# Gated linear attention in front of a mixture of experts: the attention stage rewritten around an order computed by a list scheduler

## The chip, the cores and the metric

The kernel runs on one core of one Trainium2 chip. The core has five engines with a queue each: PE (matrix products), DVE (vector), ACT (scalar and activation), POOL (GpSimd) and SP, which here only issues transfers. They work at once and wait for one another by semaphores. The metric is device microseconds of one execution: the median of several runs. The profile is one separate execution.

## The reference

The attention is a recurrence over 768 tokens, for 4 sequences and 8 heads of 48 channels. The experts take its output; every token goes to one of 8 experts, with 384 tokens for each, assigned greedily by logit.

```python
for t in range(S):                                   # S = 768, D = 48
    state = alpha[:, :, t, :, None] * state + einsum('bhd,bhe->bhde', k[:, :, t], v[:, :, t])
    y[:, :, t] = einsum('bhd,bhde->bhe', q[:, :, t], state)

x = y.transpose(0, 2, 1, 3).reshape(B * S, H * D)    # 3072 x 384
logits = x @ w_gate                                  # 8 experts
order = argsort(-logits.flatten())                   # token, expert; full experts and assigned tokens skipped
for e in range(E):
    h = maximum(x[mask_e] @ w1[e], 0)                # 384 -> 1024
    out[mask_e] = h @ w2[e]                          # 1024 -> 384
```

## The kernel before

**Steps.** The attention works in chunks of 128 tokens. A step `s` takes two heads (one above the other in 64-partition halves) and four chunks; `g, p = divmod(s, 4)` names the group of four chunks and the pair of heads. There are 24 steps, and every sixth chunk ends a sequence. One step loads four arrays of 256 KB (`load`, `load_v`, on SP's queue, three steps ahead, four buffers each) and does:

- `decay` (L221 to L224): a backward scan of `alpha` on DVE gives `sc`, a reciprocal of each chunk's first value goes into `d1f`, and a forward scan gives `ga`. The scans are 517 wide, each chunk padded to 129, so that a zero stops the running product at its end. Both of a scan's operands lie in SBUF.
- `scale_k` on DVE (L229) and `scale_q` on POOL (L235): `kh = k * sc`, `qh = q * ga`.
- `keys` (L241, L243): four transposes of `kh` on PE, copied out by ACT as `kn`.
- `scores` (L250): eight products of 64 rows on PE; `causal` (L258, L259): per head a copy by ACT and a triangular mask in place on POOL.
- `states` (L269): the products of keys and values of each chunk; `carry` (L282, L287, L289): DVE adds them to the decayed state of the pair, and ACT writes the decayed state into a block-diagonal tile `sb`, one instruction for each chunk and head, 160 in all.
- `outputs` (L296, L302): the carried state by `qh`, then the scores by the values, into one PSUM bank `y`; `emit` (L310) copies it out as `yt`.
- `logits` (L315 to L320): four products with the gate's weights into PSUM, added by DVE into `lt`. After each group `choose` transposes `lt` (L329), and `first_choice` (L351 to L364) finds each token's best expert and the first digit of its key; `first_counts` (L376) counts.
- `y_trans` (L339, L342): the rows of x are transposed back, copied by ACT into `xg`, and stored to DRAM on ACT's queue. These are put off: `fill` places them behind the last steps, and the search of the first expert waits for some of them in each level (`Y_IN_SEARCH`).

PSUM has eight banks: two for transposes (`psx`), four for the scores (two heads, two buffers), one for `y`, and one shared by states, logits and counts.

**Order.** The loop over `s` is written by hand, with steps two and one behind interleaved, and the framework orders each engine's queue by it. The first two steps run in halves on DVE (`first`, L407 to L414). `init_route` builds the tables of the routing between the steps.

**After the attention.** For each expert a search finds the threshold digit by digit in five levels: a compare (L503), 24 counting products (L551), a threshold (L552). `extract` makes the token list, rows are gathered by indirect DMA (L699), and `ffn1` and `ffn2` (L768, L788) run with weights split in two parts. The first threshold of the first expert (L379) needs the last logits.

Of the kernel before, what the change touches and what calls it, by code (L numbers as in the profile page):

```python
# [12 lines left out]
ROUTE_AHEAD = 3  # L13
LAST_BLOCKS = 2
WARM_UP = 10
Y_IN_SEARCH = (3, 4, 4, 3)
WARM_IN_ROUTE = (6, 4, 2, 2)
Y_BEFORE_CHOICE = 1
Y_BEFORE_LOGITS = 2
Y_BEFORE_COUNTS = 5  # L20
I32 = mybir.dt.int32
AF = mybir.ActivationFunctionType
OP = mybir.AluOpType


@with_exitstack
def gla_moe_kernel(ctx, tc, q, k, v, alpha, w_gate, w1, w2, out):
# [70 lines left out]
    def init_route():  # L98
        ib = dict(allow_small_or_imprecise_dtypes=True)
        nc.gpsimd.iota(ramp, pattern=[[-1, E]], base=E, channel_multiplier=0, **ib)  # L100
        nc.gpsimd.iota(pcol, pattern=[[0, 1]], base=0, channel_multiplier=1, **ib)
        tc.keep_in_program_order(
            nc.gpsimd.iota(iota, pattern=[[1, T], [0, U]], base=1, channel_multiplier=0, **ib))
        sh = 32
        for t, bits in enumerate(BITS):
            sh -= bits
            nc.any.memset(shifts[:, t], sh)
            nc.any.memset(masks[:, t], 2 ** bits - 1)
            nc.any.memset(scale[:, t], SC8[t])
        yield  # L110
        nc.vector.tensor_copy(ramp_b, ramp[:, None, :].to_broadcast([128, NU, E]))
        nc.any.memset(ones_c, 1.0)
        nc.any.memset(rem, float(CAP))
        nc.any.memset(pen, 0.0)
        nc.any.memset(asg, 0.0)
        yield
        nc.gpsimd.iota(cst, pattern=[[128, NU], [0, NB]], base=-N // 2, channel_multiplier=1, **ib)
        nc.gpsimd.iota(bsel, pattern=[[0, NU], [1, NB]], base=0, channel_multiplier=0, **ib)
        for t in range(nb):
            nc.gpsimd.memset(onet[t], SC8[t])  # L120
        nc.vector.tensor_scalar(pcs, pcol, SC8[nb - 1], None, op0=OP.mult)
        yield
        nc.gpsimd.affine_select(tri, ones, pattern=[[1, 128]], compare_op=OP.is_gt, fill=0.0, base=0,
                                channel_multiplier=-1)
        for c in cbuf:
            for w in range(0, NW, 2):
                tc.keep_in_program_order(nc.gpsimd.memset(c[:, w:w + 2], 0.0))
            yield
        for t in range(1, nb):
            n = iotas[t].shape[1]  # L130
            tc.keep_in_program_order(
                nc.vector.tensor_scalar(iotas[t], iota[:, :n], SC8[t], None, op0=OP.mult))
            yield
# [737 lines left out]
```

## Time and profile before

| | us |
|---|---|
| median of 3 runs (lowest, highest) | 475.99 (474.95, 479.57) |
| the profiled execution, its own time | 481.46 |
| its span, first to last instruction | 479.8 |
| last copy of `y` out of PSUM begins (L310) | 164.54 |
| first threshold of the first expert (L379) | 169.60 |
| first gather of rows (L699) | 190.45 |
| PE busy (3982 instructions) | 420.2 |
| DVE busy (868) | 291.4 |
| ACT busy (524) | 265.4 |
| POOL busy (181) | 183.2 |

How to read it: the profiled execution is one run, longer than its span by 1.7 us at the ends. Busy time of an engine is the sum of its instructions' records; on PE these overlap, since products are pipelined. A group's row gives its line and engine, output and inputs, the count, then the busy time and the mean in ns, then the engine's idle time in front of the group and what ended it. A timeline row gives start, length, engine, line, and the idle time before it in brackets. A row of waits gives who waited for what, the sum, the count and the longest.

### The profile page before, as it was taken

The numbers are of one execution on the slowest core, as the hardware profiler recorded it, in microseconds if no ns is written. First come the engines' busy times: TensorE is split into PE (matmuls) and PEld (weight loads), VectorE is DVE, ScalarE is ACT, GpSimd is POOL, SyncE is SP. The second block draws the span as 40 slices with busy tenths as digits, with TensorE's granted clock in tenths as the row PEclk, the third lists the DMA queues.
The fourth block names the chain that finished last, engine by engine and source line by source line (L and its number), as shares of the span: only waits on it lengthen the run. The fifth ranks groups of instructions, "written<-read, shape, count | busy, mean of one in ns | idle before, by whom it ended". The sixth has DMA issues, their size and how long they took to land.

```text
span 479.8 us, 10370 instructions
## 1 busy us (share of the span) xinstructions
PE 420.2 (88%) x3982; PEld 368.3 (77%) x3982; DVE 291.4 (61%) x868; ACT 265.4 (55%) x524; POOL 183.2 (38%) x181
## 2 busy tenths in 40 slices
PE   5987877888778885699899999988998999999993
PEld 3765756676657674489889998978986999999993
DVE  7998887788884257438768585774774851212210
ACT  2576677677587652562845637463444467674311
POOL 2765754567453100310542547045043135251202
PEclk8599789888998997669999999997997999999998
DMA  7566555545570067888999999998696599997201
GB/s 256 163 181 196 153 177 176 154 151 170 149 194 2 12 253 259 176 197 231 242 211 301 198 242 309 196 305 179 166 269 173 124 313 309 260 235 133 67 0 49
DMA packets 53296, 90.33 MB, mean 188 GB/s; under 512 B 3840, under 2 KB 27392, under 8 KB 53248
## 3 DMA queue, kind: packets, MB, share of 16 engines
q0 software_dynamic: 11776, 34.61, 34.0%
q1 hardware_dynamic: 38304, 50.35, 33.1%
q10 hardware_dynamic: 3168, 4.72, 2.7%
q8 instruction: 31, 0.51, 0.4%
q14 instruction: 17, 0.14, 0.1%
HBM read 55.06 MB, written 9.44 MB: 134 GB/s over the span
## 4 chain that ended last, share of the span: by engine, by line
PE 56%; DVE 14%; DMA 12%; issue 9%; ACT 4%; POOL 2%; another core or an unknown queue 1%; SPq 0%; POOLq 0%; ACTq 0%; DVEq 0%
PE h L768 19%; PE y L788 17%; PE rt L551 5%; DMA al<-in_alpha_dram 5%; DVE sc L221 4%; PE y L302 3%; PE y L296 3%; DVE ga L224 2%; DMA raw_k<-in_k_dram 2%; DMA w1lo<-w1r 2%; PE xt L339 1%; PE xt L752 1%; DMA w1r<-in_moe_w_dram 1%; PE s L250 1%; DVE st L289 1%
## 5 line engine op out<-in xcount | busy, mean ns | idle before, releaser
L772 ACT ACTIVATE hh<-h 128x384 fp32r<-128x384 f32 x64 | 31.0, 487 | 85.4 <-PE h L768 72.5
L773 DVE SCALAR_TENSOR_TENSOR hl<-h,hh 128x384 fp32r<-128x384 f32 x64 | 35.4, 554 | 62.7 <-ACT hh L772 58.6
L282 ACT ACTIVATE sb<-st,sc 64x48 f32<-64x48 f32 x160 | 53.1, 332 | 30.1 <-DVE st L289 12.1
L259 POOL TENSOR_SCALAR_AFFINE_SELECT sm<-sm 128x512 f32<-128x512 f32 x48 | 43.4, 924 | 67.7 <-ACT sm L258 67.7
L788 PE MATMUL y<-w2hi,hh 128*128 128x384 f32 x192 | 67.3, 350 | 1.5 <-ACT hh L772 1.5
L788 PE MATMUL y<-w2hi,hl 128*128 128x384 f32 x192 | 66.7, 348 | 0.0
L788 PE MATMUL y<-w2lo,hh 128*128 128x384 f32 x192 | 66.4, 346 | 0.0
L768 PE MATMUL h<-xh,w1lo 128*128 128x384 f32 x192 | 49.9, 361 | 1.6 <-DMA w1lo<-w1r 1.6
L699 POOL DMA_INDIRECT xr<-x_dram,idx x24 | 31.3, 1306 | 52.3 <-DVE val L630 31.2
L799 POOL DMA_INDIRECT out_dram<-yt,idx x24 | 28.2, 1174 | 60.4 <-ACT yt L792 55.5
L768 PE MATMUL h<-xl,w1hi 128*128 128x384 f32 x192 | 49.0, 357 | 0.0
L768 PE MATMUL h<-xh,w1hi 128*128 128x384 f32 x192 | 48.2, 355 | 0.2 <-ACT w2lo L728 0.2
L727 ACT ACTIVATE w1hi<-w1r 128x768 fp32r<-128x768 f32 x32 | 26.8, 839 | 35.8 <-DMA w1r<-in_moe_w_dram 14.2
L732 POOL DMA_DIRECT2D w1lo<-w1r x16 | 22.1, 1379 | 56.0 <-ACT w1lo L728 44.3
L768 PEld LDWEIGHTS h<-xh,w1lo 128*128 128x128 f32 x192 | 36.4, 201 | 5.8 <-issue 3.7
L788 PEld LDWEIGHTS y<-w2hi,hh 128*128 128x128 f32 x192 | 36.8, 192 | 2.6 <-ACT hh L772 1.8
L768 PEld LDWEIGHTS h<-xl,w1hi 128*128 128x128 f32 x192 | 35.9, 199 | 2.8 <-issue 2.6
L788 PEld LDWEIGHTS y<-w2lo,hh 128*128 128x128 f32 x192 | 37.0, 193 | 0.0
L788 PEld LDWEIGHTS y<-w2hi,hl 128*128 128x128 f32 x192 | 36.9, 192 | 0.1
L221 DVE TENSOR_TENSOR_SCAN sc<-al,d1r 128x517 f32<-128x517 f32 x22 | 32.7, 1486 | 6.0 <-DMA al<-in_alpha_dram 3.2
L302 PE MATMUL y<-sm,vt 128*48 128x128 f32 (+1 forms) x384 | 36.2, 312 | 0.0
L768 PEld LDWEIGHTS h<-xh,w1hi 128*128 128x128 f32 x192 | 35.4, 197 | 1.0 <-ACT w2lo L728 0.6
(171 smaller groups left out, 874.7 us busy)
## 6 DMA issues: line engine op xcount, KB each, us to landing
w1r<-in_moe_w_dram SPq DMA_DIRECT2D x16, 768.0 KB, 8.1
w2r<-in_moe_w_dram SPq DMA_DIRECT2D x16, 768.0 KB, 7.2
w1lo<-w1r POOLq DMA_DIRECT2D x16, 768.0 KB
w2lo<-w2r POOLq DMA_DIRECT2D x16, 768.0 KB
al<-in_alpha_dram SPq DMA_DIRECT2D x24, 256.0 KB, 3.3
raw_k<-in_k_dram SPq DMA_DIRECT2D x24, 256.0 KB, 5.3
raw_q<-in_q_dram SPq DMA_DIRECT2D x24, 256.0 KB, 4.0
vt<-in_v_dram SPq DMA_DIRECT2D x24, 256.0 KB, 2.6
```

Of the source, the lines that this page charges most:

```text
L221: nc.vector.tensor_tensor_scan(sc[:, ::-1], a[:, ::-1], d1r[:, ::-1], 1.0, op0=OP.mult, op1=OP.add)
L259: nc.gpsimd.affine_select(SM[s][:, h], SM[s][:, h], pattern=[[0, 4], [1, C]], compare_op=OP.is_ge, fill=0.0, base=0, channel_multiplier=-1)
L282: nc.scalar.activation(SB[s, u][hs, h, :D], St[p][hs], AF.Copy, scale=ac[hs])
L302: yield lambda u=u, h=h, n=n: nc.tensor.matmul(o[64 * h:64 * h + n, u], VT[s][:, u, h, :n], SM[s][:, h, u], start=False, stop=(u == 3), sk ...
L551: nc.tensor.matmul(cnt, cmp[:, j // U, :, j % U], o[:, j], start=(j == 0), stop=(j == NU - 1))
L699: last_gather[0] = nc.gpsimd.indirect_dma_start(out=XR[i][:, b], out_offset=None, in_=x_dram, in_offset=bass.IndirectOffsetOnAxis(ap=IDX[i ...
L727: nc.scalar.activation(hi[ix_], raw_[ix_], AF.Copy)
L768: nc.tensor.matmul(o, a[:, d], x[:, d], start=(n == 0), stop=(n == 3 * DB - 1))
L772: nc.scalar.activation(hh, o, AF.Relu)
L773: nc.vector.scalar_tensor_tensor(hl, o, 0.0, hh, op0=OP.max, op1=OP.subtract)
L788: F2[i, q] = nc.tensor.matmul(Y[b], a[:, bs], w, start=(q == 0 and n == 0), stop=(q == FB - 1 and n == 2))
L799: st_ = nc.gpsimd.indirect_dma_start(out=out, out_offset=bass.IndirectOffsetOnAxis(ap=IDX[i][:, b:b + 1], axis=0), in_=yt, in_offset=None)
```

## The change

The attention stage is written again, as a list of operations with an engine, an assumed cost, and the data each reads and writes. The list is ordered by a scheduler that runs while the program is built, and the order is kept as it is on all five queues (`manual_schedule` with PE, DVE, ACT, POOL and SP). The experts' stage is unchanged but for the search of the first expert, which no longer waits for row transposes.

The scheduler gives every operation a rank (the longest path behind it, plus `pl.base`, 4.4 us for each step still to come) and, going forward in time with the assumed costs, starts on each engine the operation of highest rank among those that can start within 0.1 us of the first. Buffers are rings that are handed out in the same pass.

```diff
+class Plan:
+    def add(self, eng, cost, fn, r=(), w=(), lat=None, port=False):
...
+    def order(self):
...
+            rank[i] = cost + max([rank[j] + (lat if ops[j][0] != eng else 0.0) for j in after[i]], default=0.0)
+        rank = [x + op[7] for x, op in zip(rank, ops)]
...
+            eng, t0 = min(((e, min(x)[0]) for e, x in first.items()), key=lambda x: x[1])
+            t, i = min(((t, i) for t, i in first[eng] if t <= t0 + SLACK), key=lambda x: (-rank[x[1]], x[0]))
...
+HOP = {"PE": 0.3, "DVE": 0.15, "ACT": 0.2, "POOL": 0.2, "SP": 2.2}
+SLACK = 0.1
```

Buffers and banks. PSUM now holds one bank for all transposes (`xt`: keys, rows, logits and counts), one for small products `m` (`dvb`), two for the scores of both heads, one each for `y`, states and logits, and one for the scan's second operand `zb`.

```diff
+    RA, RK, RQ = (ring(6, [128, w], n) for n, w in (("al", AW), ("rk", 4 * C), ("rq", 4 * C)))
+    RV = ring(6, [128, 4, 2, D], "rv")
+    TE, TP = ring(3, [128, 4 * C], "te"), ring(2, [128, 4 * C], "tp")
+    KH, QH = ring(3, [128, 4, C], "kh"), ring(4, [128, 4, C], "qh")
+    KN, SM = ring(2, [128, 4, C], "kn"), ring(2, [128, 2, 4, C], "sm")
+    SB = ring(2, [128, 4, 2, 64], "sb")
+    YT, XG = ring(4, [128, 4, C], "yt"), ring(2, [128, 4, Dm], "xg")
...
+    XT = Kind([bank("xt", [128, 4, C], psx)], ordered=False)
+    dvb = bank("xt", [128, 4, C], psx).rearrange("p a b -> p (a b)")
+    SC, YB, ST, LG = (Kind([bank(n, [128, x, 4, C] if x > 1 else [128, 4, C])])
+                      for n, x in (("s", 2), ("y", 1), ("st", 1), ("lg", 1)))
+    zb = bank("z", [128, 4 * C])
+    MR = Kind([dvb[:, 12 * i:12 * i + 12].rearrange("p (u c) -> p u c", c=3) for i in range(6)])
```

Scans and scaling. The host sets the first `alpha` of each chunk to zero, so the scans are 512 wide without padding, and hands the true first values over in 12 more columns of the same array. The first two steps run in halves; `kh` and `qh` are made on DVE for step 0 and on POOL after it.

```diff
+            def scan_e(lo=lo, top=top):
+                nc.vector.tensor_tensor_scan(te.t[:, lo:top][:, ::-1], al.t[:, lo + 1:top + 1][:, ::-1],
+                                             zb[:, lo + 1:top + 1][:, ::-1], 1.0, op0=OP.mult, op1=OP.add)
+            def scan_p(lo=lo, hi=hi):
+                nc.vector.tensor_tensor_scan(tp.t[:, lo:hi], al.t[:, lo:hi], zb[:, lo:hi], 1.0,
+                                             op0=OP.mult, op1=OP.add)
+            def ends(us=us, lo=lo, hi=hi, n=n):
+                a0 = al.t[:, 4 * C + 1:4 * C + 13].rearrange("p (u c) -> p u c", c=3)
+                nc.vector.tensor_tensor(m.t[:, us], a0[:, us], te.t[:, lo:hi:C][:, :, None].to_broadcast([128, n, 3]),
+                                        op=OP.mult)
...
+            ek, ck, en = (V, 0.08 + 0.15 * n, nc.vector) if s == 0 else (G_, 0.06 + 0.28 * n, nc.gpsimd)
+            add(ek, ck, lambda f=mul: f(en, kh, rk, te), r=each_u(te) + [rk], w=each_u(kh), port=True)
...
+            add(ek, ck, lambda f=mul: f(en, qh, rq, tp), r=each_u(tp) + [rq], w=each_u(qh), port=True)
...
+                add(V, 0.08, lambda: nc.vector.memset(zb[:, 0:4 * C:C], 1.0), w=["Z"])
```

Scores, states, outputs. One ACT copy and one POOL mask cover both heads. The states of a pair stay in five slots of one tile, and one DVE product of the slots by `m` (whose columns hold the decay for the upper head, the lower head and both) writes all eight blocks of `sb`.

```diff
+        add(P_, 0.45, turn(xt, kh), r=[(kh, u) for u in every], w=[xt])
+        add(A_, 0.6, lambda: nc.scalar.activation(kn.t, xt.t, AF.Copy), r=[xt], w=[kn])
...
+            add(P_, 0.45, score, r=[(kh, u) for u in us2] + [(qh, u) for u in us2], w=[(sc, a)])
+        add(A_, 1.05, lambda: nc.scalar.activation(sm.t, sc.t, AF.Copy), r=[(sc, 0), (sc, 1)], w=[sm])
+        add(G_, 1.15, lambda: nc.gpsimd.affine_select(
+            sm.t, sm.t, pattern=[[0, 8], [1, C]], compare_op=OP.is_ge, fill=0.0, base=0, channel_multiplier=-1),
+            w=[sm])
...
+                    slot(u + 1), slot(u), m.t[:, u, 2:3], st.t[:, u, :D], op0=OP.mult, op1=OP.add),
+                    r=[st, m], w=[("T", p)])
+        def carried():
+            t = ts[:, 4:0:-1] if g % 2 else ts[:, 0:4]
+            nc.vector.tensor_tensor(sb.t[:, :, :, :D], t[:, :, None, :].to_broadcast([128, 4, 2, D]),
+                                    m.t[:, :, :2, None].to_broadcast([128, 4, 2, D]), op=OP.mult)
...
+        add(A_, 0.6, lambda: nc.scalar.activation(yt.t, yb.t, AF.Copy), r=[yb], w=[yt])
```

Logits, rows, choice. The logits of the four pairs accumulate in PSUM and are copied once by ACT. The rows of x are transposed in each step and stored on SP's queue after each group. The choice runs in three batches (`BATCHES = ((0, 3), (3, 5), (5, 6))`, in groups) in place of six, with the compare written into the search's own buffer.

```diff
+                nc.tensor.matmul(lg.t[32 * u:32 * u + 32, 0], wg[:, p], yt.t[:, u], start=(p == 0),
+                                 stop=(p == HP - 1), skip_group_check=True)
...
+            add(P_, 0.45, turn(x3, yt), r=[yt], w=[x3])
...
+                add("SP", 3.0, lambda: nc.sync.dma_start(
+                    x_dram[4 * g * C:4 * (g + 1) * C].rearrange("(u p) d -> p u d", p=C), xg.t),
...
-                    head[0] += Y_IN_SEARCH[t - 1]
-                    order = [last_k[0], YM[head[0] - 1]]
+                    order = [last_k[0]] if last_k[0] else []
```

On the host, `v` is no longer padded (48 columns a head in place of 64), and `alpha` has 528 columns in place of 512.

More of the change, by code (lines that the diff above doesn't have):

```diff
@@ L118, in init_route @@
[L118 to L128, printed above, removed]
+            a("POOL", 0.1, lambda t=t, sh=sh: gp.memset(shifts[:, t], sh))
@@ L461, in gla_moe_kernel @@
+    ordered = dict(engines={mybir.EngineType.PE, mybir.EngineType.DVE, mybir.EngineType.Activation,
+                            mybir.EngineType.Pool, mybir.EngineType.SP})
+    with tc.manual_schedule(**ordered):
+        pl.issue()
+    if DEBUG:
+        DEBUG(pl)
     att.close()
```

624 lines of the change are left out of this document (318 added, 306 removed).

## The prediction

> **What bounds the kernel now.** I read first the page's heading and slices, then the table of stretches, then the groups of instructions of the steady part, the waits of SP's queue, and last the timeline of single blocks. The table of stretches cuts the span where the work changes: start, steady attention, attention's tail, first search, experts. Columns: the stretch, its length, busy time of each engine (instructions), granted clock, DMA share, GB/s.
>
> ```profile
> span 479.8 us, 10370 instructions
> 10.00:20.00 10.00, 9.60 (x66) 7.15 (x66) 9.90 (x22) 5.85 (x13) 8.41 (x18) 0.50 0.83 266
> 20.00:140.00 120.00, 98.68 (x1250) 79.09 (x1249) 100.08 (x220) 83.15 (x202) 69.56 (x62) 0.89 0.57 165
> 140.00:166.00 26.00, 21.57 (x267) 17.34 (x262) 11.07 (x36) 18.14 (x45) 6.92 (x8) 0.93 0.09 26
> 190.50:479.80 289.30, 267.82 (x2180) 248.29 (x2178) 147.50 (x486) 146.85 (x240) 95.88 (x80) 0.94 0.81 204
> ```
>
> The change touches only what lies before 190.5 us. From 20 to 140 us no engine is full: PE's records cover 82%, DVE 83%, and PE's records overlap one another. What sets the pace shows in the groups of 20 to 140 us, the waits of SP's queue, and the first chain row:
>
> ```profile
> L282 ACT ACTIVATE sb<-st,sc 64x48 f32<-64x48 f32 x126 | 41.9, 332 | 23.6 <-DVE st L289 10.6 <-DVE d1f L222 4.8 <-DVE val L353 2.7
> L259 POOL TENSOR_SCALAR_AFFINE_SELECT sm<-sm 128x512 f32<-128x512 f32 x38 | 36.8, 987 | 47.0 <-ACT sm L258 47.0
> L235 POOL TENSOR_TENSOR qh<-raw_q,ga 128x512 f32<-128x512 f32 x20 | 32.4, 1618 | 3.5 <-issue 2.6 <-PE y L296 0.7
> L221 DVE TENSOR_TENSOR_SCAN sc<-al,d1r 128x517 f32<-128x517 f32 x21 | 31.5, 1499 | 6.0 <-DMA al<-in_alpha_dram 3.2 <-ACT sm L258 1.5 <-ACT sb L282 1.2
> L224 DVE TENSOR_TENSOR_SCAN ga<-al,d1f 128x517 f32<-128x517 f32 x20 | 30.3, 1516 | 0.0
> L258 ACT ACTIVATE sm<-s 128x512 f32<-128x512 f32 x38 | 20.8, 600 | 0.9 <-PE s L250 0.7
> L229 DVE TENSOR_TENSOR kh<-raw_k,sc 128x512 f32<-128x512 f32 x20 | 17.9, 896 | 1.7 <-DMA raw_k<-in_k_dram 1.7
> L289 DVE SCALAR_TENSOR_TENSOR st<-st,sc,st 128x48 f32<-128x48 f32 x49 | 12.2, 249 | 2.0 <-PE st L269 1.8
> L320 DVE TENSOR_TENSOR lt<-lt,st 128x128 f32<-128x128 f32 x14 | 3.9, 278 | 5.7 <-PE st L315 5.7
> L222 DVE RECIPROCAL d1f<-sc 128x4 f32<-128x4 f32 x20 | 3.5, 173 | 0.1
> SPq L182 <- PE y L302: 77.4, 18, 8.7
> by line: DMA al<-in_alpha_dram 16.5%; DVE sc L221 11.9%; PE y L302 10.4%; PE y L296 9.2%; DVE ga L224 8.0%; DMA raw_k<-in_k_dram 7.2%; issue 5.4%; DVE st L289 3.9%; PE st L269 3.8%; ACT sb L282 3.7%; PE st L315 3.7%; DVE kh L229 2.7%; PE s
> ```
>
> Some 20 steps (20 of the 24 `ga` scans) in 120 us make 6.0 us a step. It is a loop over four engines: SP's load of `vt` waits for `outputs` of an older step on PE (77.4 us in 18 waits), the `al` load is queued behind it, the next scan waits for that, and PE, ACT and DVE hand one step on to the next. DVE's own work is about 5.0 us a step (100.08 / 20), and half a microsecond of that is contention, as the timeline shows:
>
> ```profile
> 142.69 1.22 DVE L224 TENSOR_TENSOR_SCAN ga<-al,d1f 128x517 f32<-128x517 f32 x1
> 147.04 1.21 POOL L235 TENSOR_TENSOR qh<-raw_q,ga 128x512 f32<-128x512 f32 x1 [0.30 <-PE y L296]
> 147.12 1.15 DVE L355 TENSOR_SCALAR sg<-m 128x4 int32<-128x4 int32 x1
> ```
>
> A scan alone takes 1.22 us against 1.50 on average; a four-element instruction took 1.15 us because POOL's product began just before it.
>
> **The change part by part.** *PE.* It keeps every attention product, and the 24 row transposes (`y_trans`), most of which ran between 160 and 183 us, move into the steps. The price of a block is the start of the next minus its own start, where they follow without a wait, at full clock (timeline of PE, 154 to 161 us):
>
> ```profile
> 154.63 0.66 PE L241 MATMUL xt<-ident,kh 128*128 128x128 f32 x4
> 155.22 1.16 PE L250 MATMUL s<-qh,kh 64*128 64x128 f32 x16
> 157.08 0.42 PE L315 MATMUL st<-yt,wg 128*32 128x128 f32 x8 [0.70 <-ACT yt L310]
> 157.44 0.94 PE L296 MATMUL y<-qh,sb 128*128 128x128 f32 x6
> 158.30 0.47 PE L269 MATMUL st<-vt,kn 128*48 128x48 f32 x12
> 158.71 0.49 PE L296 MATMUL y<-qh,sb 128*128 128x128 f32 x2
> 159.12 1.08 PE L302 MATMUL y<-sm,vt 128*48 128x128 f32 x16
> 160.13 1.09 PE L339 MATMUL xt<-ident,yt 128*128 128x128 f32 x8
> ```
>
> Over 24 steps: key transposes 0.59 x 24 = 14.2; scores 1.16 x 24 = 27.8; logits 0.36 x 24 = 8.6; carried products 0.86/6 x 160 records (80 chunks carry a state, two records a product) = 22.9; states 0.41/12 x 320 = 10.9; scores by values 1.01 x 24 = 24.2; row transposes 1.09/8 x 96 = 13.1. Sum 122 us, 5.07 a step. The lower bound is the weight loads' own time, 79.09/20 = 4.0 a step, plus 0.55 for the row transposes: 4.5, or 109 us. I take 122: the gaps between blocks of unlike shape recur in the rows wherever the shape changes, and the change keeps the shapes.
>
> *DVE.* Removed: `kh` (0.90; now on POOL from the second step), `lt` (0.28; logits accumulate in PSUM), contention on two scans. Added: the product that makes `m` (`ends`), a memset, `carried`. A step: scans 2 x 1.22, reciprocal 0.17, `ends` 0.17 (the row nearest in size is the reciprocal), memset 0.1 (under the reciprocal), states 3.33 x 0.25 = 0.83, `carried` with 384 elements between `lt`'s 0.28 (128) and `kh`'s 0.90 (512, contended), taken 0.5. That is 4.2, or 100 us; the s=0 products 1.8, three batches of choice (about 33 small instructions at 0.17 and the wide compare) 8, six table instructions at 0.5 or less, 2.5: 112. That a scan reads its second operand from PSUM at the old price no row shows; the bounds are 1.22 (alone) and 1.50 (as now), so 0 to +13 us; I take 0, since `lt` at 128 elements with a PSUM operand costs 0.28, of one kind with SBUF rows.
>
> `ends` still takes two SBUF operands. Bounds from the rows above: 0, or a wait for a whole POOL product, 24 x 1.2 = 29 us. I take a third, 10. DVE 122 us.
>
> *POOL.* `kh`, `qh`, one wide mask: 2 x 1.21 plus twice the mask's shortest, 0.63:
>
> ```profile
> L259 POOL TENSOR_SCALAR_AFFINE_SELECT sm<-sm x48: 632/692/1568, 11.6 to 158.7; 128x512 f32<-128x512 f32 x48
> L235 POOL TENSOR_TENSOR qh<-raw_q,ga x21: 1177/1609/2228, 23.1 to 147.0; 128x512 f32<-128x512 f32 x21
> ```
>
> 3.7 a step, 89 us; at today's contended means (1.62, 1.62, 2 x 0.99) 5.2, 125 us. Off the path at the first. *ACT* loses 160 `sb` instructions (160 x 0.332 = 53 us) and keeps two mask halves, `kn` and `yt` at 0.6 and the rows' copy at 0.5: 2.9 a step, covered.
>
> ```profile
> L243 ACT ACTIVATE kn<-xt 128x512 f32<-128x512 f32 x19 | 11.3, 595 | 0.3
> 165.12 0.49 ACT L342 ACTIVATE xg<-xt 128x384 f32<-128x384 f32 x1
> ```
>
>
> *DMA.* Loads are now 128 x (528+512+512+384) x 4 B = 0.99 MB a step, 23.8 MB, and x's six stores (4.7 MB) move from ACT's queue and the search into the steps, on SP's queue. The queue's row (packets, MB, share of 16 engines) gives the rate:
>
> ```profile
> q1 hardware_dynamic: 38304, 50.35, 33.1%
> ```
>
> 50.35 MB in 33.1% of 479.8 us is 317 GB/s, so 28.5 MB take 90 us, hidden under 122. Six buffers in place of four let loads run five steps ahead, which covers a store of x that waits for its rows at the head of SP's queue; the 77 us of `vt` waits lose their effect.
>
> *Start and tail.* The last rows needed, from the timeline: the first score, `yt` of the last step, the first threshold, the second search level and the first gather.
>
> ```profile
> 7.47 0.88 PE L250 MATMUL s<-qh,kh 64*128 64x128 f32 x8 [2.24 <-DVE qh L414]
> 164.54 0.60 ACT L310 ACTIVATE yt<-y 128x512 f32<-128x512 f32 x1 [1.86 <-PE y L302]
> 169.60 0.17 DVE L379 TENSOR_TENSOR g<-st,need 128x8 bf16<-128x8 f32 x1 [1.11 <-PE st L376]
> 173.96 1.03 DVE L503 TENSOR_TENSOR cmp<-nd,iota 128x768 bf16<-128x768 bf16 x2
> 175.50 0.94 PE L551 MATMUL rt<-o,cmp 128*128 128x8 bf16 x24
> 190.45 1.17 POOL L699 DMA_INDIRECT xr<-x_dram,idx  x1 [31.15 <-DVE val L630]
> ```
>
> The first step is still halved on DVE, so PE starts near 7.5. It starts cold: the row of 10 to 20 us has clock 0.50. The bounds of that cost are 0 and half of 7.5 to 20 us, 6; I take 6, since PE has steps waiting from the second on. PE's waits for others I put at 5 us (4% of 122); the bounds are 0 and the third rival below. The last `yt` then ends at 7.5 + 122 + 6 + 5 + 0.6 = 141.1, less logits and row transposes behind it (0.36 + 0.55): 140.2, against 165.1 now. Gain 24.9. DVE stands just under: 4.4 + 122 + one step's chain of some 7 = 133. From `yt` to the threshold (169.60) lie the same steps as now, 4.5 us.
>
> In the search the compare ends at 174.99 and the counts start at 175.50, behind row transposes; without them three levels save 0.5 each, 1.5. Their cover for the clock goes too: 24 counts take 0.94, twice that at half clock, in four levels 0 to 3.8 us more. I take 0, since the search's own products and the spins before the experts remain. The gather at 190.45 keeps 20 us from the last store of x, so the store moves nothing.
>
> *The sum.* 24.9 + 1.5 = 26.4 less than the profiled execution's 481.5 (span 479.8 and 1.7 around it): 455. That execution lies 5.5 above the median of the runs shown, 475.99, so the median should be 476 - 26 = **450 us**.
>
> *Two rules weighed.* DVE's contention: the rows are the scan at 1.22 or 1.50 and the 1.15 us behind POOL. The Trainium skill, "SBUF — State Buffer", section "Who interferes with whom", says that a VectorE instruction with at most one SBUF input stays clear of GpSimd, while one with two SBUF inputs waits for the whole GpSimd instruction. By it the scans go at 1.22, as in my sum, but it speaks against `ends`, where it gives the second rival. The clock: the row is 9.60 us of PE work in 10 at clock 0.50. The skill's "TensorE: Matmul & The Clock Gate", Part 1, has the clock full after one busy window of about 3.4 us; by that the 6 us fall away and the time would be 444. This case's row disagrees, so I keep the 6.
>
> **The rivals.** *First: PE packs tighter, 435 us.* If the gaps between unlike blocks close when nothing waits, PE needs 4.5 a step, 109 us, and DVE without stalls on `ends` 112. The change ranks its work by 4.4 us a step. The last `yt` comes at 4.4 + 112 + 7, plus waits of 2: 125, 40 less; with the search 41. For it: no engine's hard work is over 4.7. Against: the gaps stand in every row above.
>
> *Second: DVE becomes the bound, 463 us.* If `ends` waits for POOL's product each time, DVE needs 112 + 29 = 141, and `yt` ends at 4.4 + 141 + 7 = 152: 13 less. For it: the 1.15 us row; POOL is busy 3.7 of each 5 us, and `qh` becomes ready just as `ends` does. Against: whoever is first goes first, and `ends` needs only DVE's own work.
>
> *Third: slower, 490 us.* PSUM becomes single: scores of both heads had two buffers and get one, the transposes' two banks become one, and both transposes of a step share it. PE then stops for ACT's evictions unless another block is ready in its fixed order. The price: 1.1 (mask copy), 0.6 (`kn`), 0.5 (rows), 0.6 (`yt`), 2.8 us a step if none is covered. It decides at 6.1 a step, where PE works 5.07 of it: with 1.0 uncovered the gain is gone; with 1.6 uncovered the step is 6.7, 24 x 0.6 = 14 us over now. For it: PE works only 4.5 of 6.0 today, with more PSUM. Against: today's waits are the load loop's, and ACT sheds 2.2 us a step.
>
> **How the numbers follow.** Chances: forecast (441 to 460) 0.50; first rival 0.20; second 0.12; no gain, 471 to 481, the third rival at its turning point, 0.10; third rival above 481, 0.08. A measurement of this kernel tells about 1% from no change: faster by over 1% is 0.82, within 1% 0.10, slower 0.08. The range leaves out the no-gain and slower cases: 428 to 468, which takes in the first two rivals.
>
> **What would show it.** Right: PE records over 90% in 30 to 130 us at clock 1.0, steps of 5.0 to 5.3 us, scans at 1.2, no wait of SP for PE products in front of loads, the last `yt` near 140 and the first gather near 164. First rival: steps of 4.5. Second: `ends` with a mean near 1 us. Third: PE's idle time put down to ACT `sm`, `kn` or `yt`. The prediction is wrong in its main step if PE waits over 1 us a step, or if the experts' stage, now 289 us from the first gather to the end, changes by more than a few us.

## The result and the profile after

The changed kernel takes 456.76 us, median of 3 runs (454.44 to 457.65), against 475.99 before: a ratio of 0.956, 95% interval 0.949 to 0.963. In a later set it took 454.76 us (451.93 to 457.41, 6 runs) against 467.06 for the kernel before (the median of 6 of its 11 runs, which went from 463.17 to 476.9): 0.973, 0.967 to 0.980. Ratios, here and in the experiments, leave out runs more than 1.5% above the fastest of the same kernel in the set, while medians and ranges in the experiments' table take in all runs, and the profiles of e1 and e4 are of runs that the ratios leave out. So the changed kernel is faster by 2.7 to 4.4%, some 12 to 19 us.

The profiled execution of the changed kernel took 456.76 us, with a span of 455.0. First its heading and engines, from the page:

```profile
span 455.0 us, 10123 instructions
PE 400.8 (88%) x3982; PEld 351.1 (77%) x3982; DVE 281.8 (62%) x828; ACT 213.0 (47%) x349; POOL 186.3 (41%) x196
```

ACT lost 175 instructions and 52 us, as the removal of the 160 `sb` instructions said; PE has the same 3982 matrix products. Then the table of stretches for the start and the steady part, with the columns of before:

```profile
10.00:20.00 10.00, 3.15 (x26) 2.36 (x28) 9.44 (x21) 0.69 (x2) 2.71 (x3) 1.00 0.31 97
30.00:130.00 100.00, 96.41 (x1305) 77.11 (x1299) 86.95 (x185) 51.74 (x85) 70.48 (x59) 1.00 0.63 214
```

The first row is the surprise. PE was busy for 9.60 of these 10 us before; now it stands for most of them, while DVE is at 9.44. The second row is the forecast: PE is dense. The same stretch for the line of the scores alone gives the length of a step:

```profile
30.00:130.00 100.00, 26.46 (x320) 20.39 (x320) 1.00 0.63 214
```

A step has 16 score products, so 320 of them are 20 steps in 100 us: 5.0 us a step, 6.0 before. The groups of DVE and POOL from the start to 165 us (group, busy time, mean ns, idle time before it) show what became cheaper:

```profile
L352 DVE TENSOR_TENSOR_SCAN tp<-al,z 128x512 f32<-128x512 f32 x22 | 26.8, 1217 | 1.4 <-POOL qh L361 0.6
L348 DVE TENSOR_TENSOR_SCAN te<-al,z 128x511 f32<-128x511 f32 x22 | 26.8, 1216 | 0.5
L357 DVE TENSOR_TENSOR xt<-al,te 128x12 f32<-128x12 f32 x22 | 11.3, 514 | 0.6
...
L361 POOL TENSOR_TENSOR qh<-rq,tp 128x512 f32<-128x512 f32 x22 | 28.0, 1273 | 0.4 <-DVE z L372 0.4
L361 POOL TENSOR_TENSOR kh<-rk,te 128x512 f32<-128x512 f32 x22 | 28.0, 1273 | 7.2 <-DMA rk<-in_k_dram 2.5 <-DVE z L366 2.5 <-DVE te L348 1.6
L392 POOL TENSOR_SCALAR_AFFINE_SELECT sm<-sm 128x1024 f32<-128x1024 f32 x24 | 26.6, 1108 | 38.2 <-ACT sm L391 34.6 <-DVE ts L413 3.6
```

The scans, 1.50 us before, take 1.22, and POOL's product 1.27 where it took 1.62. One DVE instruction with two SBUF operands is left, `ends` (named `xt<-al,te` here): 12 elements in 0.514 us on average, against 0.186 for the reciprocal.

Why PE starts late shows in the timelines of SP and DVE:

```profile
0.83 2.77 SPq L324 DMA_DIRECT2D al<-in_alpha_dram  x6
3.64 0.43 SPq L324 DMA_DIRECT2D rk<-in_k_dram  x1
```

```profile
5.05 0.73 DVE L249 TENSOR_SCALAR iota<-iota 128x512 bf16<-128x512 bf16 x2 [2.24 <-POOL iota L231]
...
6.26 0.69 DVE L348 TENSOR_TENSOR_SCAN te<-al,z 128x256 f32<-128x256 f32 x1
...
9.55 0.69 DVE L348 TENSOR_TENSOR_SCAN te<-al,z 128x256 f32<-128x256 f32 x1
...
12.85 1.22 DVE L348 TENSOR_TENSOR_SCAN te<-al,z 128x511 f32<-128x511 f32 x1
14.10 0.19 DVE L366 RECIPROCAL z<-te 128x4 f32<-128x4 f32 x1
14.19 1.83 DVE L361 TENSOR_TENSOR kh<-rk,te 128x256 f32<-128x256 f32 x2
```

The scans share one second operand, `zb`, so in the list they form a chain through all 24 steps; the rank of a scan holds the rest of that chain, and the rank of the first `kh` a shorter path. So SP issues six `al` loads before the first `rk`, and DVE makes tables of the search first (5.05, waiting 2.24 us for POOL), then the scans of steps 0 and 1 and the first of step 2 (12.85), and only then `kh` of step 0 (14.19). PE's first product, the last copy of `y` and the first gather follow, from the timelines of PE, ACT and POOL:

```profile
16.17 1.09 PE L377 MATMUL xt<-ident,kh 128*128 128x128 f32 x4 [10.32 <-DVE xt L357]
```

```profile
147.58 0.60 ACT L437 ACTIVATE yt<-y 128x512 f32<-128x512 f32 x1 [1.43 <-PE y L434]
```

```profile
171.97 1.24 POOL L779 DMA_INDIRECT xr<-x_dram,idx  x1 [31.21 <-DVE val L710]
```

PE's first product of the attention was the first score at 7.47 before. The last `yt` begins 17.0 us earlier than before (164.54), the gather 18.5 earlier (190.45). From the gather to the end are 283.0 us, 289.4 before.

### The profile page after: what moved, and what is told of

The parts are those of the page before. It is cut to its first block, busy times and chain, and to the rows that moved or that the text cites. A ratio compares the mean times of both kernels' runs of the same rounds, so it can differ in the third digit from the quotient of the medians.

```text
span 455.0 us, 10123 instructions
## 1 busy us (share of the span) xinstructions
PE 400.8 (88%) x3982; PEld 351.1 (77%) x3982; DVE 281.8 (62%) x828; ACT 213.0 (47%) x349; POOL 186.3 (41%) x196
## 3 DMA queue, kind: packets, MB, share of 16 engines
HBM read 53.69 MB, written 9.44 MB: 139 GB/s over the span
## 4 chain that ended last, share of the span: by engine, by line
PE 67%; DVE 10%; issue 9%; DMA 5%; ACT 3%; POOL 2%; another core or an unknown queue 1%; SPq 1%; POOLq 0%; DVEq 0%; ACTq 0%
PE y L868 18%; PE h L848 18%; PE s L389 6%; PE rt L631 5%; PE xt L377 5%; PE y L434 5%; PE y L427 4%; DMA w2lo<-w2r 3%; PE st L401 2%; DVE cmp L584 2%; PE xt L832 1%; DVE te L348 1%; PE lg L445 1%; PE xt L772 1%; DMA rq<-in_q_dram 1%
## 5 line engine op out<-in xcount | busy, mean ns | idle before, releaser
L779 POOL DMA_INDIRECT xr<-x_dram,idx x24 | 31.3, 1305 | 51.2 <-DVE val L710 31.2
L848 PE MATMUL h<-xh,w1lo 128*128 128x384 f32 x192 | 47.5, 347 | 1.5 <-DMA w1lo<-w1r 1.5
L848 PE MATMUL h<-xl,w1hi 128*128 128x384 f32 x192 | 47.7, 349 | 0.2 <-DVE xl L837 0.2
L848 PE MATMUL h<-xh,w1hi 128*128 128x384 f32 x192 | 46.4, 344 | 0.2 <-DVE hl L853 0.2
L392 POOL TENSOR_SCALAR_AFFINE_SELECT sm<-sm 128x1024 f32<-128x1024 f32 x24 | 26.6, 1108 | 38.2 <-ACT sm L391 34.6
L631 PEld LDWEIGHTS <-cmp 128*128 128x128 bf16 x816 | 30.6, 118 | 12.8 <-DVE cmp L584 9.7
L631 PE MATMUL rt<-o,cmp 128*128 128x8 bf16 x816 | 33.1, 175 | 6.3 <-DVE cmp L584 6.3
L848 PEld LDWEIGHTS h<-xh,w1lo 128*128 128x128 f32 x192 | 34.6, 192 | 4.5 <-issue 2.5
L848 PEld LDWEIGHTS h<-xl,w1hi 128*128 128x128 f32 x192 | 34.5, 192 | 3.3 <-issue 2.7
L812 POOL DMA_DIRECT2D w2lo<-w2r x16 | 15.3, 956 | 49.2 <-ACT w2lo L808 48.5
L848 PEld LDWEIGHTS h<-xh,w1hi 128*128 128x128 f32 x192 | 34.1, 190 | 1.2 <-ACT xh L835 0.7
```

What stands on the lines that cost most here:

```text
L392: add(G_, 1.15, lambda: nc.gpsimd.affine_select(sm.t, sm.t, pattern=[[0, 8], [1, C]], compare_op=OP.is_ge, fill=0.0, base=0, channel_multi ...
L631: nc.tensor.matmul(cnt, cmp[:, j // U, :, j % U], o[:, j], start=(j == 0), stop=(j == NU - 1))
L779: last_gather[0] = nc.gpsimd.indirect_dma_start(out=XR[i][:, b], out_offset=None, in_=x_dram, in_offset=bass.IndirectOffsetOnAxis(ap=IDX[i ...
L812: nc.gpsimd.dma_start(lo.bitcast(F32), raw_, accum_op=OP.add, max_dma_last_dim=8192)
L848: nc.tensor.matmul(o, a[:, d], x[:, d], start=(n == 0), stop=(n == 3 * DB - 1))
```

## The experiments

Three marks are read from each run's profile: the first key transposition on PE, the start of the last copy of `y`, and the start of the first gather. Where all else is equal, the copy of `y` is the end of the attention. The marks of the changed kernel came out the same in two profiles (16.2, 147.6, 172.0), so a shift of 2 us in them can be read, where one in the time can't: the stretch from the gather to the end, whose code is the same in every kernel here, took from 277.7 to 289.4 us. e1 to e4, e5 to e8, and a0 to e12 ran each on one chip, with the kernel before between them (476.76, 476.85 and 469.07 us, medians of 7, 7 and 11; of those that the ratios use, 469.64, 476.85 and 467.06).

| run | what is edited | median (range) of all runs, us | ratio to before (95%) | first key | last `y` | gather | gather to end |
|---|---|---|---|---|---|---|---|
| before | | 475.99 (474.95–479.57) | | 7.5 (score) | 164.5 | 190.4 | 289.4 |
| after | | 456.76 (454.44–457.65) | 0.956 (0.949–0.963) | 16.2 | 147.6 | 172.0 | 283.0 |
| e1 | first steps ranked first | 459.97 (454.99–463.75) | 0.972 (0.954–0.989) | 10.0 | 148.7 | 173.1 | 288.9 |
| e2 | `ends` from PSUM | 455.53 (452.77–458.57) | 0.970 (0.956–0.984) | 16.2 | 145.5 | 169.9 | 281.2 |
| e3 | whole blocks | 460.76 (456.12–465.01) | 0.978 (0.962–0.994) | 15.8 | 145.7 | 170.1 | 284.3 |
| e4 | +13 us on PE | 468.21 (461.55–472.97) | 0.990 (0.958–1.021) | 16.2 | 158.5 | 182.9 | 288.3 |
| e5 | `zb` in SBUF | 485.13 (482.51–488.19) | 1.019 (1.012–1.026) | 17.0 | 172.6 | 196.9 | 286.3 |
| e6 | before, loads six ahead | 486.25 (480.4–489.21) | 1.017 (1.008–1.025) | | 173.0 | 198.9 | 285.6 |
| e7 | +13 us on DVE | 465.05 (464.57–465.52) | 0.976 (0.968–0.985) | 16.2 | 155.5 | 179.9 | 283.9 |
| e8 | e1, e2, e3 together | 460.16 (458.3–461.7) | 0.966 (0.960–0.972) | 10.0 | 146.2 | 170.6 | 288.5 |
| a0 | after, unedited | 454.76 (451.93–457.41) | 0.973 (0.967–0.980) | 16.2 | 147.6 | 172.0 | 282.9 |
| e10 | measured costs in the plan | 450.67 (449.93–453.59) | 0.967 (0.962–0.973) | 16.7 | 145.3 | 169.6 | 278.9 |
| e11 | e2, measured costs | 451.05 (450.08–457.07) | 0.970 (0.963–0.978) | 16.7 | 146.3 | 170.7 | 277.7 |
| e12 | e8, measured costs, tables later | 444.80 (441.24–446.67) | 0.951 (0.946–0.957) | 7.5 | 139.3 | 163.7 | 281.3 |

### What the PSUM operand of the scans is worth

```diff
-    zb = bank("z", [128, 4 * C])
+    zb = ap_.tile([128, 4 * C], F32, name="z")
```

> One part of the change undone: the scans' second operand lies in SBUF again in place of PSUM, all else and the order unchanged. Theory (the PSUM operand takes the scans out of POOL's way and DVE is one of the two bounds): the scans' mean rises from 1.22 to 1.4 to 1.55, POOL's products from 1.27 to 1.5 or more, the last copy of y moves to 157 to 170, time 465 to 478. Rival (the scans' price does not matter, PE is the bound): within 3 us of the changed kernel.

Groups of DVE and POOL of this run, with the same columns and stretch as above:

```profile
L348 DVE TENSOR_TENSOR_SCAN te<-al,z 128x511 f32<-128x511 f32 x22 | 38.0, 1728 | 0.5
L352 DVE TENSOR_TENSOR_SCAN tp<-al,z 128x512 f32<-128x512 f32 x22 | 37.9, 1722 | 2.0 <-POOL qh L361 1.1
...
L361 POOL TENSOR_TENSOR qh<-rq,tp 128x512 f32<-128x512 f32 x22 | 38.9, 1768 | 1.5 <-DVE z L372 1.2 <-DVE xt L357 0.3
...
L392 POOL TENSOR_SCALAR_AFFINE_SELECT sm<-sm 128x1024 f32<-128x1024 f32 x24 | 34.4, 1433 | 34.0 <-ACT sm L391 33.3 <-DMA rk<-in_k_dram 0.6
```

And its stretch from 30 to 130 us, where the changed kernel has 1305 products:

```profile
30.00:130.00 100.00, 84.88 (x1088) 66.61 (x1088) 94.53 (x159) 42.96 (x70) 83.89 (x52) 0.97 0.59 198
```

Each scan grows by 0.51 us (44 of them: 22.3 us), POOL's `qh` by 0.50 and its mask by 0.33, and the last copy of `y` comes 25.0 us later, beyond the theory's 157 to 170: the kernel becomes slower than before. DVE works 128.1 of the 140 us from 10 to 150, against 112.1. So with both operands in SBUF the scans and POOL's instructions hold each other up, and the operand's place is the largest part of the change that was tried by itself: without it the rest of the change, as planned here, gains nothing. How much that rest is worth alone with the operand in PSUM was not tried part by part.

### Whether the loads paced the kernel before

The kernel before, with seven buffers in place of four and loads six steps ahead:

```diff
-    RB = 4
+    RB = 7
...
-            load(nm, s + 3)
+            load(nm, s + 6)
```

> The kernel before with seven buffers for each loaded array in place of four, and loads six steps ahead in place of three; nothing else. Theory (the loop through SP, where the load of vt waits for an older step's products and the alpha load stands behind it, sets the pace of the kernel before): scans no longer wait for alpha, steps go from 6.0 to some 5.3 us, time falls by 8 to 16 us. Rival (the hand-offs between PE, ACT and DVE set the pace and the loads only follow): time within 4 us of the kernel before.

Waits of its SP queue and DVE, 10 to 175 us (who waits for whom: sum, times, longest), then a group of DVE:

```profile
SPq L182 <- PE y L302: 70.7, 16, 7.9
```

```profile
DVE sc L221 <- ACT sb L282: 18.3, 14, 2.2
```

```profile
L221 DVE TENSOR_TENSOR_SCAN sc<-al,d1r 128x517 f32<-128x517 f32 x22 | 27.7, 1259 | 18.4 <-ACT sb L282 18.3
```

It is slower by 1.7%, where one theory had it faster and the other the same, and its last `y` comes 8.5 us later. SP still waits for PE almost as long, only further ahead: its queue stands in front of buffers that aren't free, and no engine waits for a load any more. The scan no longer waits for `al`, but for ACT's `sb`, which reads the decay, 18.3 us in 14 waits. The loop over SP in the prediction was not what set the step; the prediction's own row of this scan (L221) has only 3.2 us of waiting for `al`. The backward scan also takes 1.26 us here, where it took 1.49 in the kernel before, and the attention is no faster for it.

### Adding work to PE, and to DVE

In e4 the key transposes run twice, in e7 DVE's `carried` product:

```diff
+                if src is kh:
+                    for u in range(4):
+                        nc.tensor.transpose(dst.t[:, u], src.t[:, u], ident)
```

> The four key transposes of each step are made twice into the same bank, 96 more PE transposes of about 0.14 us each, with the order unchanged. The output stays the reference's. Theory (PE is the bound of the whole stage): time up by 24 x 0.55 = 13 us, less what falls into the waits that PE has, so 466 to 471. Rival (another engine or the hand-offs set the pace): up by 0 to 5 us.

```diff
+        def twice():
+            carried()
+            carried()
-        add(V, 0.5, carried, r=[("T", p), m], w=[sb])
+        add(V, 0.5, twice, r=[("T", p), m], w=[sb])
```

> The product that spreads the states (carried) is made twice, 24 more DVE instructions of 0.55 us, with the order unchanged; the counterpart on DVE to the doubled transposes on PE, which moved the last copy of y by 11 of 13 us. Theory now (PE and DVE are both bounds: PE waits for kh, qh and sb, DVE waits in its fixed order for PE's states, so a delay on either is paid nearly in full and a relief of one alone is not): the last copy of y moves from 147.6 to 155 to 161, time up by 7 to 13 us. Rival (PE alone is the bound): up by 0 to 4 us.

Some 13 us more on PE (24 x 0.55) move the last copy of `y` by 10.9; 13.2 more on DVE (24 x 0.55) move it by 7.9. If PE alone were the bound, these would be 13 and nearly 0. So more work on either engine moves the end, and what one loses in its fixed order the other makes up only in part. Since `carried` stands between PE's states and PE's next products, e7 can't tell DVE's load from the length of that chain: PE's waits for `sb` sum to 8.1 us in e7, and to 3.9 in the changed kernel.

### Taking work off DVE and PE

In e2 the twelve-element product `ends` reads one of its two operands from PSUM: the four chunk values are copied there first.

```diff
-                nc.vector.tensor_tensor(m.t[:, us], a0[:, us], te.t[:, lo:hi:C][:, :, None].to_broadcast([128, n, 3]),
+                nc.vector.tensor_copy(m.t[:, us, 3], te.t[:, lo:hi:C])
+                nc.vector.tensor_tensor(m.t[:, us, :3], a0[:, us], m.t[:, us, 3:4].to_broadcast([128, n, 3]),
```

> The small product that makes m (ends) reads its second operand from PSUM, after a copy of four values per step into PSUM, in place of two SBUF operands. Theory (the mean of 0.51 us for it is POOL's products in front of it, and PE is the bound): the product's mean falls to 0.17 to 0.20 us, DVE loses some 7 us of busy time and gets 24 copies of about 0.17, and since DVE is not the bound the time falls by only 0 to 3 us (454 to 457). Rival (DVE bounds the stage): the time falls by 5 to 8 us, 449 to 452.

The two groups of DVE in this run:

```profile
L358 DVE TENSOR_TENSOR xt<-al,xt 128x12 f32<-128x12 f32 x22 | 3.8, 175 | 0.8
L357 DVE COPY xt<-te 128x4 f32<-128x4 f32 x22 | 3.6, 162 | 0.6
```

The product falls from 0.514 to 0.175 us, so 22 x 0.34 = 7.5 us of it was contention with POOL. With the copy's 3.6, DVE saves 3.9, and the last `y` comes 2.1 earlier. The time, 455.53, lies in the first theory's range, and can't be told from that of the changed kernel. The mean of 0.514 hides two kinds, as rows of the changed kernel's timeline show:

```profile
63.20 0.18 DVE L357 TENSOR_TENSOR xt<-al,te 128x12 f32<-128x12 f32 x1
64.76 3.26 DVE L357 TENSOR_TENSOR xt<-al,te 128x12 f32<-128x12 f32 x3
```

Nine of the 22 full-size products took 0.68 us or more, up to 1.21, and thirteen took 0.15 to 0.19; the three that start at 64.76 run while POOL works without a break.

In e3 the scores and the intra-chunk products go to PE as whole blocks of 16 and not as halves.

```diff
-        for a in range(2):
-            us2 = (2 * a, 2 * a + 1)
+        for a in range(1):
+            us2 = (0, 1, 2, 3)
```

> The scores and the products of scores by values are one block each per step in place of two halves. Theory (PE is the bound, and each change of shape between blocks costs it about 0.17 us: a half of the scores takes 0.65 from start to next start and the whole 1.09, a half of the other 0.57 and the whole 1.01): PE's records shrink by up to 0.33 us a step, time 449 to 454. Rival (the order's freedom is worth more than the gaps: half blocks let ACT and POOL start earlier): the time rises, 458 to 465.

The last `y` comes 1.9 earlier, and 0.4 of that PE already has at its start (15.8 against 16.2). The time, 460.76, falls in the rival's range, but with runs from 456.12 to 465.01 it decides nothing.

### Starting PE early

In e1 the planner's base of the first three steps is raised, so that their `kh` and loads outrank the scans of later steps.

```diff
-        pl.base = 4.4 * (NS - s)
+        pl.base = 4.4 * (NS - s) + (60.0 * (3 - s) if s < 3 else 0.0)
```

> The ranks of the first three steps are raised so that their loads and DVE work go step by step (alpha, k, v, q of step 0 first; kh of step 0 ahead of the scans of step 1), everything else as in the changed kernel. Theory (the 8 us missing from the forecast are PE's late start, 16.2 us in place of 7.5, and PE bounds the stage from its first block on): PE starts at 8 to 10 us, the last copy of y ends 6 to 9 us earlier (148.2 now, 139 to 142 then), time 448 to 451. Rival (DVE or POOL bounds the stage, and PE would only wait later): PE starts early too, but the last copy of y stays within 3 us of 148, time 454 to 457.

The ranks were what held PE back: it starts at 10.0 in place of 16.2. But the attention ends no earlier (148.7 against 147.6), as the rival had it. With e2 and e3 added, e8 was meant to show whether the three add up:

> The three edits together: the first three steps in step order, the product for m without two SBUF operands, scores and values products as whole blocks. Theory (two bounds): alone the edits moved the last copy of y (147.6) by +1.1, -2.1 and -1.9; together they relieve both engines and the early start of PE can be used, so more than the sum of the parts: last copy of y at 136 to 142, time 445 to 451. Rival (something else, as the order itself or ACT, paces the stage): the sum of the parts, last copy at 144 to 146, time 452 to 456.

They don't do more than that: the last `y` comes at 146.2, near the sum of the parts that the rival had, and the time is no better. The stretch from 10 to 40 us, for the changed kernel, e1 and e8, in this order:

```profile
10.00:40.00 30.00, 21.88 (x267) 17.67 (x268) 26.09 (x60) 10.13 (x15) 16.65 (x16) 1.00 0.53 169
```

```profile
10.00:40.00 30.00, 26.52 (x316) 21.51 (x316) 27.23 (x61) 12.69 (x19) 19.88 (x19) 0.87 0.57 184
```

```profile
10.00:40.00 30.00, 23.89 (x270) 19.13 (x270) 25.60 (x67) 11.87 (x17) 18.56 (x18) 0.81 0.59 190
```

In e8 PE starts 6.2 us earlier and has done 270 products by 40 us, where the changed kernel has done 267: the head start is gone, though at 36 us it was still 47 products. In e1 it is worth 49 products at 40 us, under one step (65), and is lost later. The place of the loss in e8 is a pair of waits in its timeline of PE, while DVE makes four scans in a row (33.39 to 38.92) in front of the `ts` that PE needs:

```profile
37.69 0.66 PE L378 MATMUL xt<-ident,yt 128*128 128x128 f32 x4 [1.08 <-ACT kn L382]
40.21 0.47 PE L402 MATMUL st<-rv,kn 128*48 128x48 f32 x12 [1.87 <-DVE ts L414]
40.67 0.94 PE L428 MATMUL y<-qh,sb 128*128 128x128 f32 x6
41.54 1.63 PE L435 MATMUL y<-sm,rv 128*48 128x128 f32 x16
42.95 0.70 PE L402 MATMUL st<-rv,kn 128*48 128x48 f32 x12
43.58 1.98 PE L390 MATMUL s<-qh,kh 64*128 64x128 f32 x16
```

After the waits come slow blocks as well: 1.63 for 1.08, 1.98 for 1.16. The half clock returns behind them.

### The durations in the plan

The planner's costs sum to 4.0 us of PE work for an average step (4.2, as the expectation has it, for one with all four chunks), where 5.0 are measured; for `ends` it has 0.16, where 0.51 are. In e10 only the planner's costs, and the base of its rank, are set by the measured ones; the instructions are the same, and their order changes. In e11 this goes with e2; in e12 with e8, and with the tables of the search held back until the scans of step 1.

```diff
-            add(V, 0.06 + 0.275 * n, scan_e, r=[al], w=each_u(te) + ["Z"])
+            add(V, 0.06 + 0.29 * n, scan_e, r=[al], w=each_u(te) + ["Z"])
...
-        add(P_, 0.45, turn(xt, kh), r=[(kh, u) for u in every], w=[xt])
+        add(P_, 0.55, turn(xt, kh), r=[(kh, u) for u in every], w=[xt])
...
-            add(P_, 0.45, score, r=[(kh, u) for u in us2] + [(qh, u) for u in us2], w=[(sc, a)])
+            add(P_, 0.6, score, r=[(kh, u) for u in us2] + [(qh, u) for u in us2], w=[(sc, a)])
...
-        pl.base = 4.4 * (NS - s)
+        pl.base = 5.0 * (NS - s)
```

and, in e12 alone, beside e8's edits:

```diff
-            add(eng, cost, fn, r=r, w=["init%d" % n[0]])
+            add(eng, cost, fn, r=[*r, "go"], w=["init%d" % n[0]])
...
-            add(V, 0.06 + 0.29 * n, scan_p, r=[al, "Z"], w=each_u(tp))
+            add(V, 0.06 + 0.29 * n, scan_p, r=[al, "Z"], w=each_u(tp) + (["go"] if s == 1 else []))
```

> The changed kernel itself, nothing edited, beside the three others of this set on the same chip, so that their marks and times stand against it directly. Marks expected as in its first profile: first key transposition at 16.2 us, last copy of y at 147.6, first gather at 172.0. The stretch from the first gather to the end has been 281 to 289 us in the profiles so far, in kernels whose code for it is the same; here it may be anywhere in that band, and the median in 452 to 462 us.

> Only the planner's durations are changed, to those that the trace shows: a PE step of 4.2 us in the plan becomes 5.0, a scan 1.16 becomes 1.22, ends 0.16 becomes 0.53, a POOL product 1.18 becomes 1.28; the rank's base grows from 4.4 to 5.0 a step. The instructions are the same, only their order on the queues changes. Theory one, that PE and DVE lose the 8 us beyond their bounds because the order was laid out for a PE that is faster than the real one (so that DVE, which works strictly in that order, stands behind products of PE that come later than planned): last copy of y at 141 to 145 us, 3 to 6 us off the time. Theory two, that the chain between DVE, POOL and PE sets the pace whatever the order: last copy of y within 1.5 us of 147.6, and no change in the time. The start does not change by this: first key transposition stays near 16.

> The ends read from PSUM alone (as in the second run of the set before, which ended its last copy of y at 145.5) with the measured durations in the plan. Theory one: last copy of y at 139 to 143 us, time 4 to 8 us under the changed kernel. Theory two: 145 to 146 us, time 2 us under it.

> Everything together: first three steps ranked first, the tables of the search made after the scans of the second step, ends from PSUM, scores and intra-chunk products as whole blocks, and the measured durations in the plan. First key transposition at 10 us or before. Theory one, that the bad plan wasted the early start of the set before (which ended its last y at 146.2): 10 + 24 steps of 5.0 + 5 for the half clock at the start + some 3 at the end = 138 us, so last copy of y at 135 to 141 and a median 7 to 12 us under the changed kernel. Theory two: last copy of y at 144 to 147, median within 3 us of the changed kernel.

e10 lies between the two theories: the last `y` at 145.3, 2.3 earlier, and in time 4.1 us under a0 with ranges that touch. e11 adds nothing to it (146.3, where the first theory had 139 to 143 and the second 145 to 146): with PE starting at 16.7, order and `ends` together are worth 1 to 2 us, not more. e12 lands where the first theory put it: the last `y` at 139.3, in 135 to 141, and its median 10.0 us under a0, with no overlap of the runs. Its rows of DVE's first scan, PE's first product, the first 30 us and the last `y`:

```profile
3.80 0.69 DVE L348 TENSOR_TENSOR_SCAN te<-al,z 128x256 f32<-128x256 f32 x1 [0.99 <-DMA al<-in_alpha_dram]
```

```profile
7.53 0.69 PE L378 MATMUL xt<-ident,kh 128*128 128x128 f32 x4 [2.08 <-DVE kh L362]
```

```profile
10.00:40.00 30.00, 26.30 (x334) 21.46 (x331) 25.90 (x63) 13.15 (x20) 25.58 (x33) 0.86 0.70 225
```

```profile
139.34 0.60 ACT L438 ACTIVATE yt<-y 128x512 f32<-128x512 f32 x1 [1.43 <-PE y L435]
```

PE has done 334 products by 40 us, 67 or one whole step more than in the changed kernel. Its first product comes 2.5 us earlier than e8's (7.5 against 10.0), for DVE's first scan no longer stands behind the tables (3.80 against 6.26). How the 6.9 us between the last `y` of e8 and of e12 divide between that start, the rest of the tables' move and the measured costs, no run separates. e12 is the fastest kernel here, 22 us under the kernel before in its set (467.06).

## Why the prediction was right, and where it missed

**The time.** 450 was forecast, 456.76 measured, in the range of 428 to 468 and in the forecast's own band of 441 to 460. The sum had 26.4 us; the gather came 18.5 earlier, and the median 19.2. The main mechanism held: PE packed densely at 5.0 us a step, with the scans at 1.22.

**The step that failed is the start.** "The first step is still halved on DVE, so PE starts near 7.5": PE started at 16.17, 8.7 later. The last `yt` was to end at 140.2 and ended at 148.2, 8.0 later. From PE's first product to that end the sum had 140.2 - 7.5 = 132.7; the profile has 148.2 - 16.2 = 132.0. That these agree so well is partly luck: PE's records cover 125.0 of the 132.0, so it waited 7.0 where 5 was taken, and the half clock cost about 3.4 where 6 was taken. The working looked at the row of before and at the diff's halves, but not at what the rank does in the first steps: the `Z` entries, which chain the scans, stand in the diff's operations. e1 and e8 show that the miss is not undone by starting PE alone; e12, with the start at 7.5, ends its last `yt` at 139.9 and gathers at 163.7 (forecast: near 164), though it also holds e2 and e3.

**PE's step.** 5.07 forecast, 5.0 measured; PE's records cover 96.4% from 30 to 130 us. That the change keeps the shapes was not exact: it halves the scores and the intra-chunk products, and e3, which makes them whole and changes the order with it, ends 1.9 us earlier.

**The half clock.** 6 us were taken, from bounds of 0 and 6. The changed kernel's timeline of PE shows where it ended:

```profile
22.85 0.88 PE L401 MATMUL st<-rv,kn 128*48 128x48 f32 x16
23.66 0.99 PE L427 MATMUL y<-qh,sb 128*128 128x128 f32 x6
24.59 1.08 PE L434 MATMUL y<-sm,rv 128*48 128x128 f32 x16
25.50 0.53 PE L401 MATMUL st<-rv,kn 128*48 128x48 f32 x16
```

From one start to the next the states take 0.81 at 22.85 and 0.45 at 25.50; the block at 23.66 takes 0.93 and the one at 24.59 takes 0.91, near the 0.86 and 1.01 of the prediction's rows at full clock. So from 16.17 to about 23.7, less 0.69 of waiting, blocks ran at nearly twice their length: some 3.4 us lost. The Trainium skill, "TensorE: Matmul & The Clock Gate", Part 1, has the full clock after some 3.4 us of sustained work; half of that, an estimate by the page, is 1.7 lost. By the blocks here it took 7.5 us, the last 5.7 of them behind the one pause of 0.69, so this trace, too, shows longer than the page.

**DVE.** The scans were put at 1.22 and measured 1.217; `ends` was given 10 us of contention, and e2 shows 7.5. The rule of the Trainium skill's "SBUF — State Buffer", "Who interferes with whom", did hold here in both directions: one SBUF operand 1.22, two 1.72 (e5), and the twelve-element product 0.175 against 0.514. That each `ends` would wait for the whole POOL instruction, as the second rival had it, didn't happen: nine of 22 were held, up to 1.21 us, and the mean is 0.51.

**PE as the bound, with DVE just under.** Only half right. DVE was weighed as a sum of its own, to be compared with PE's; in e4 and e7, 13 us more on PE and on DVE's chain cost 10.9 and 7.9, and PE's longest waits in the changed kernel, 3.9 of the 7.0 us, are for DVE's `sb`. The last scan ends at 130.2 and the last `yt` 18 us later, not 7: at the end DVE is done and PE still holds over three steps.

**POOL, search, single PSUM buffers.** POOL's step is 2 x 1.273 + 1.108 = 3.65 (3.7 forecast). From the threshold to the gather the search saves 1.5 (20.85 to 19.4), the forecast's figure. PE's waits for ACT's copies sum to about 1 us each for `sm`, `kn` and `xg`, so the third rival's mechanism is nearly absent.

**What paced the kernel before.** The account, SP's wait for `outputs` handed down through `al` to the scan, was wrong: in e6 no engine waits for a load any more, and the kernel gets slower. What set its step instead stays open. In the changed kernel the scans' contention with POOL, which the prediction had booked inside DVE's sum, is worth 25.0 us (e5); but in e6 the backward scan loses most of its contention (1.49 to 1.26 us) and the time doesn't fall, so contention alone was not what held the kernel before; the scan's 18.3 us of waiting for ACT's `sb` point to the hand-offs between the engines, which no run tests further. The right step length came from PE's own sum, which doesn't need that account.

**The experts' stage.** It was to change by no more than a few us. It is 6.4 shorter in these two profiles, but with the same code it took 277.7 to 289.4 in the others, so no effect of the change is read from it.

## What to carry to other kernels

In a scheduled kernel, read the first microseconds separately: here a serial chain through all steps outranked the one product that lets the busiest engine begin, and PE began 8.7 us later than forecast. Two engines near full in a fixed order are not two bounds of which the larger counts: here a microsecond more on either cost 0.6 to 0.8, and single repairs gave some 2 us or nothing until start, order and the two small edits came together. A mean can hide two kinds: 0.51 us for `ends` was 0.18 or about 1. A long wait in a queue's row shows who stands, not who is waited for: more buffers are the test.

## What the runs showed of the hardware

- Moving one operand of a 128x512 scan from SBUF to PSUM is worth 0.51 us on each scan beside POOL (1.72 to 1.22, e5 and the changed kernel), and 0.50 on POOL's 128x512 product (1.77 to 1.27).
- The granted clock of a stretch can hide the half clock. From 10 to 30 us the changed kernel's two profiles, first this one, then a0, have the same work and the same marks, at 1.00 and at 0.66:

```profile
10.00:30.00 20.00, 11.99 (x132) 9.78 (x132) 16.66 (x42) 4.82 (x7) 8.74 (x9) 1.00 0.46 142
```

```profile
10.00:30.00 20.00, 11.89 (x132) 9.71 (x132) 16.66 (x42) 4.82 (x7) 8.73 (x9) 0.66 0.48 147
```

  The blocks' lengths tell it in both: the score block at 19.80 takes 2.08 us, and the one near 25.9 takes 1.16.
- The half clock came back in e8 behind waits of 1.08 and 1.87 us within four (scores at 1.98), and in e1 behind one of 1.78 (`y` products at 2.08 for 1.16), but not in the changed kernel, where PE waited 2.13 us before 69.64 and the next block took its usual 1.16. So the length of one wait doesn't decide it; what does is open.
- A twelve-element DVE product with two SBUF operands takes 0.15 to 0.19 us or up to 1.21 in the same kernel, and 0.175 on average in e2, where one operand lies in PSUM.
